# Both broadcasts of a group of head pairs in one place, the last reciprocals ahead of operand tiles, and two side-by-side products that end one after the other

## The chip, the cores and the metric

The kernel runs on one core of one Trainium2 chip. Its time is the device time of one execution in microseconds (us), as the median of several runs. PE is the matrix engine (TensorE), DVE the vector engine, ACT the scalar engine, POOL the GpSimd engine; SP only issues DMAs here. Each engine works through its own instructions in order, and semaphores tie the engines together.

## The reference

Attention with a tanh cap on the scores, then a gated layer with RMS normalisation, then a second layer with a leaky activation:

```
scores = cap * tanh(q @ k.T / 8 / cap)        # 2 batches x 12 heads, 448 x 64
attn   = exp(scores - max); attn /= attn.sum(-1) + 1e-9
x      = (attn @ v) as 896 x 768
xn     = x / sqrt(mean(x * x) + 1e-6) * rms_g
y      = (silu(xn @ w_gate) * (xn @ w_val)) @ w_out        # 768 -> 1536 -> 768
h      = y @ w_in                                          # 768 -> 2048
out    = (max(h, 0) + alpha * min(h, 0)) @ w_out2          # 2048 -> 768
```

## The kernel before

The attention comes first. Heads go two by two: 12 **pairs** (6 for each batch element), and each pair takes two **bursts**, numbered 0 to 23, so that pair i has bursts 2i and 2i + 1. A burst is: PE makes the scores of two key blocks (`qk`, L189), ACT applies tanh and exp (`soft`, L199 and L201, output `pt`), and PE multiplies the `pt` of the burst before with the values (`pv`, L212, into `oo`). Beside this skeleton two tables of numbers, `early` (filled by `ahead`, emitted between `qk` and `soft`) and `later` (filled by `at`, emitted at the end of the burst), say in which burst each other step is emitted.

A pair is divided by its softmax sums in these steps. In burst 2i + 2 PE sums the exponentials (`sums`, L228, into the PSUM bank `u`), DVE copies the unnormalised output (`evac_o`, L254, tile `ee`) and the sums (`evac_u`, L262, tile `us`), and SP spreads the sums over partitions by two small DMAs (tile `gt`). Two pairs make a **group**; `recip` (L269) works on a whole group with four small DVE instructions (L274 to L281: add, reciprocal, high part `th`, remainder `tl`) and two DMAs that bring the result into the rows `r`. `norm` (L306) is PE's broadcast of such a row over the partitions (L310, `rps<-r`) and DVE's product (L311, `xf<-ee,rps`). `norm` always used the bank `r`, but for the two at burst 23 and the one of pair 10, which share out `r` and `u`. POOL squares and adds up each finished pair (`square`, L292 to L300).

For the first batch element `rms_sum` (PE, L330), `rms_root` (ACT, L335, which loads a table for the square root) and `rms_tail` (DVE, L338, a reciprocal over 448 columns) give the RMS factor, and `xnorm` (L351 to L358) makes the high and low parts `xh`, `xl` of the operand tiles that the first products of the next stage read.

The products of the dense layers run as three-term sums of high and low parts: `wh` (ACT, L120) and `wl` (DVE, L124) are a weight block, and seven block products P1 to P7 per group of output columns follow Strassen's and Winograd's scheme; POOL forms the sums S1 to S4 of weight blocks (L115). `product` (L378) does one. `products` (L390) does the first two kinds, P5 and then P6, for two output groups side by side, so that the low operand part is read last. P6 and P7 share PSUM banks: between them DVE takes P6 out (`u2`, L562, `b<-s,c`), and P7 (operand T3, from `later_operands`) goes on in the same banks. A second planner (`do(slot, rank, ...)`) hangs such steps on the slots of the dense stage.

Pairs 8, 9 and 10 are divided at the very end, and pair 11 is divided without the detour over DMA (`norm_now`, with bank `r` for its sums).

Of the kernel before, what the change touches and what calls it, by code (L numbers as in the profile page):

```python
# [54 lines left out]
def attn_moe_kernel(ctx: ExitStack, tc: tile.TileContext, units, qk_in, v, sel, w, gvec, alpha, cap, out):  # L55
# [87 lines left out]
    def sum3(lay, g):  # L143

        w_sum((lay, g, "S3"), (lay, g, "A22"), (lay, g, "S2"), ALU.subtract, home=(lay, g, "A21"))
# [5 lines left out]
    def sum4(lay, g):  # L151

        w_sum((lay, g, "S4"), (lay, g, "A12"), (lay, g, "S2"), ALU.subtract, home=(lay, g, "A12"))
# [115 lines left out]
    def recip(n):  # L269
        t = gt.pop(n)  # L270
        w = 2 * len(members[n])
        m = slice(0, w * RP)
        f = sb.tile([4 * RP, S // RP], F32, tag="gf", name="gf")
        nc.vector.scalar_tensor_tensor(  # L274
            out=f[m], in0=t[m, 0], scalar=eps_t[m], in1=t[m, 1], op0=ALU.add, op1=ALU.add
        )
        nc.vector.reciprocal(out=f[m], in_=f[m])
        th = sb.tile([4 * RP, S // RP], F32R, tag="th", name="th")
        tl = sb.tile([4 * RP, S // RP], F32R, tag="tl", name="tl")
        nc.vector.tensor_copy(th[m], f[m])  # L280
        nc.vector.tensor_tensor(out=tl[m], in0=f[m], in1=th[m], op=ALU.subtract)  # L281
        rr = r2[n % 2]
        for r0, x in ((0, th), (32, tl)):
            row = rr[r0:r0 + w].rearrange("r (p s) -> r p s", p=RP)
            nc.sync.dma_start(out=row.bitcast(F32), in_=x[m].bitcast(F32))
# [27 lines left out]
    def norm_now(i):  # L313

        b, p = divmod(i, NP)
        u = sb.tile([P, S], F32, tag="us", name="us")
        nc.vector.tensor_scalar_add(u, us.pop(i)[:, :S], eps_t)
        nc.vector.reciprocal(out=u, in_=u)
        nc.vector.tensor_tensor(out=xf[b][:, p, :], in0=oo.pop(i)[:, :S], in1=u, op=ALU.mult)
        square(i)  # L320
# [5 lines left out]
    def rms_sum(b):  # L326
        ms = ms_of[b] = ps_o.tile([P, 512], F32, tag="o", name="ms")
        parts = s2.pop(b)
        for n, t in enumerate(parts):
            nc.tensor.matmul(ms[:, :S], ones, t, start=n == 0, stop=n == len(parts) - 1)  # L330
# [6 lines left out]
    def rms_tail(b):  # L337
        nc.vector.reciprocal(out=rstd[b], in_=rstd[b])  # L338
# [9 lines left out]
    def xnorm(i, late=None):  # L348
        b, p = divmod(i, NP)
        x = xf[b][:, p, :]  # L350
        nc.vector.scalar_tensor_tensor(  # L351
            out=x, in0=x, scalar=g_t[:, p:p + 1], in1=rstd[b], op0=ALU.mult, op1=ALU.mult
        )
        if b == 0:
            h, l = first_operand("B21" if p >= K3 else "B11")
            if late is None:
                nc.vector.tensor_copy(h[:, p % K3, :], x)
                nc.vector.tensor_tensor(out=l[:, p % K3, :], in0=x, in1=h[:, p % K3, :], op=ALU.subtract)  # L358
            else:
                nc.scalar.copy(h[:, p % K3, :], x)  # L360
                late.append((l[:, p % K3, :], x, h[:, p % K3, :]))

    def lows(late):
        for o, x, h in late:
            nc.vector.tensor_tensor(out=o, in0=x, in1=h, op=ALU.subtract)
        del late[:]
# [16 lines left out]
    def products(pss, us, name):  # L383

        xh, xl = oper[name]
        mm = [(p, x, k) for k in range(K3) for p, x in ((h_t, xh), (l_t, xh))] + [(h_t, xl, k) for k in range(K3)]
        for n, (wt, x, k) in enumerate(mm):
            for ps, u in zip(pss, us):
                for r in range(2):
                    nc.tensor.matmul(  # L390
                        ps[:, r, :S], wt[u][:, r * K3 + k, :], x[:, k, :], start=n == 0, stop=n == len(mm) - 1,
                        skip_group_check=True,
                    )


    with tc.manual_schedule():
# [39 lines left out]
        def at(n, fn, *a):  # L436
            later.setdefault(n, []).append((fn, a))

        def ahead(n, fn, *a):
            early.setdefault(n, []).append((fn, a))  # L440
# [6 lines left out]
        for i in range(NPAIR):  # L447
            e = 2 * i
            at(e, prep, i + 1)
            at(e, load_raw, i + 2)  # L450
            at(e, load_v, i + 1)
            if i > 0:
                at(e, sums, i - 1)
                if i % 2 == 1 and i > 2:
                    at(e, recip, (i - 3) // 2)
                if i - 2 in range(len(conv)):
                    at(e, w_bits, conv[i - 2])
                    if i - 2 < len(conv) - RAW:
                        at(e, w_next, conv[i - 2])
                if i == 10:  # L460
                    at(e, rms_tail, 0)
                at(e, evac_o, i - 1)
                at(e, evac_u, i - 1)
            if i in range(3, last):
                ahead(e + 1, norm, i - 3)
                at(e + 1, square, i - 3)
            if i - 1 in range(len(conv)):
                at(e + 1, w_top, conv[i - 1])
        for i in (last - 3, last - 2):
            ahead(NA - 1, norm, i, "ru"[i - last + 3])  # L470
        for n, j in ((6, 0), (8, 1), (18, 6), (22, 7)):
            at(n, w_hi, conv[j])
            if j < 7:
                at(n + 1, w_lo, conv[j])
        for n, fn, g in ((13, sum1, 0), (15, sum1, 1), (17, sum2, 0), (19, sum2, 1), (21, sum3, 0)):
            at(n, fn, "g", g)
        at(18, rms_sum, 0)
        at(19, rms_root, 0)
        for m in range(3):
            at((21, 21, 22)[m], xnorm, m)  # L480
        for n in range(NA):
            i, b = bursts[n]
            for g in (2 * b, 2 * b + 1):
# [15 lines left out]
        def ct(name):  # L499
            return xpool.tile([P, 2, S], F32, tag="ct", name=name, bufs=2)  # L500
# [3 lines left out]
        def first_sum(g, home):  # L504

            c21[g] = home
            nc.scalar.copy(home, pa[g][:, :, :S])  # L507
# [4 lines left out]
        square(last - 3)  # L512
        square(last - 2)
        recip(len(members) - 1)
        late = []
        xnorm(NP - 3, late)
        lows(late)
        norm_now(last)
        for g in (1, 0):
            (sum3 if g else sum4)("g", g)  # L520
        product(pa[0], ("g", 0, "A11"), "B11", True, rows=(0,))
        norm(last - 1, "u")
        square(last - 1)
        product(pa[0], ("g", 0, "A11"), "B11", True, rows=(1,))
        xnorm(NP - 2, late)
        xnorm(NP - 1, late)
        lows(late)
        rms_sum(B - 1)
        first_sum(0, ct("c21"))
        rms_root(B - 1)  # L530
        w_hi(("g", 0, "S1"))
        w_lo(("g", 1, "A12"))
        sum4("g", 1)
        rms_tail(B - 1)
        product(pa[1], ("g", 1, "A11"), "B11", True)
        first_sum(1, ct("c21"))
        w_hi(("g", 1, "S1"))
        c11 = [spare[B - 1][:, :2], xpool.tile([P, 2, S], F32, tag="B22l", name="c11")]
# [256 lines left out]
        def later_operands(n0, steps):  # L795
            for name, at_sum, at_hi, out, a, b in steps:
                if a is not None:
                    do(n0 + at_sum, 5, tt, out, a, b, ALU.subtract)
                do(n0 + at_hi, 5, operand, name, out)
                do(n0 + at_hi + 1, 2, operand_low, name, out)  # L800

        b11, b12, b21, b22 = x0[:, lo3], x1[:, lo3], x0[:, hi3], x1[:, hi3]
        later_operands(0, (
# [212 lines left out]
```

## Time and profile before

| | us |
|---|---|
| median of 3 runs | 592.72 (592.49 to 594.05) |
| profiled execution, its own time | 599.0 |
| span of the profiled execution | 597.2 |

PE is busy for 97% of the span, DVE for 66%, ACT for 57%, POOL for 19%. The mean granted clock of PE is 0.992 of full speed. A share of PE that high leaves some 19 us in which PE does nothing, 5.4 us of it before the first matmul and 4.3 us behind the last. So the places in the middle where PE waits, or runs at a lower clock, are few, and they can be read one by one. All stretches below are in us from the span's start, in the time of this one profiled execution.

### The profile page before, as it was taken

How to read it: one execution, taken by the hardware profiler on the slowest of the kernel's cores; microseconds unless marked ns; L12 is line 12 of the kernel's file. 1: busy time of each engine (PE TensorE's matmuls, PEld its weight loads, DVE VectorE, ACT ScalarE, POOL GpSimd, SP SyncE). 2: the span in 40 equal slices, each digit the busy share in tenths (PEclk: the TensorE clock that was granted, in tenths of full speed). 3: DMA queues.
4: the chain of work that ended last, by engine and by line, in shares of the span. 5: the costliest groups of instructions: out<-in, count | busy, mean ns of one | idle time of the engine just before them, and what ended most of it. 6: DMA issues, size and time to landing. Idle time of an engine off the chain costs nothing.

```text
span 597.2 us, 7299 instructions
## 1 busy us (share of the span) xinstructions
PE 577.8 (97%) x2925; PEld 472.8 (79%) x2925; DVE 394.1 (66%) x425; ACT 341.7 (57%) x392; POOL 114.9 (19%) x60
## 2 busy tenths in 40 slices
PE   6999999899899999999999999999999999999997
PEld 3444444389699999999999999999889889999996
DVE  5568869897997696769661643969986877504100
ACT  6998889456545544447634344486775986332101
POOL 0014545410046242310000053401441000000000
PEclk9999999799999999999999999999999999999999
DMA  7655420300136334114631653004321344431002
GB/s 253 220 194 157 139 71 19 137 25 1 26 133 212 106 106 159 53 60 152 210 115 46 224 200 106 0 1 150 120 101 54 128 137 159 158 145 53 1 1 92
DMA packets 16506, 66.05 MB, mean 111 GB/s; under 512 B 3544, under 2 KB 4056, under 8 KB 16472
## 3 DMA queue, kind: packets, MB, share of 16 engines
q1 hardware_dynamic: 16184, 65.45, 32.1%
q8 instruction: 23, 0.38, 0.3%
q0 software_dynamic: 144, 0.13, 0.1%
q14 instruction: 11, 0.09, 0.1%
q10 hardware_dynamic: 144, 0.00, 0.0%
HBM read 62.66 MB, written 2.75 MB: 110 GB/s over the span
## 4 chain that ended last, share of the span: by engine, by line
PE 82%; DVE 11%; DMA 3%; issue 2%; ACT 2%; SPq 0%; ACTq 0%; DVEq 0%
PE s L378 19%; PE m L378 14%; PE s L652 6%; PE s L654 6%; PE s L656 6%; PE m L652 6%; PE m L656 5%; PE m L654 5%; PE oo L212 5%; PE s L189 4%; DVE b L562 2%; PE us L228 2%; DVE wl L124 1%; PE m L390 1%; PE s L390 1%
## 5 line engine op out<-in xcount | busy, mean ns | idle before, releaser
L124 DVE TENSOR_TENSOR wl<-wt,wh 128x768 fp32r<-128x768 f32 x98 | 105.5, 1083 | 94.4 <-ACT wh L120 94.3
L115 POOL TENSOR_TENSOR wt<-wt 128x768 f32<-128x768 f32 x40 | 92.3, 2312 | 264.4 <-DVE wt L107 148.5
L120 ACT CAST wh<-wt 128x768 fp32r<-128x768 f32 x98 | 81.2, 832 | 89.7 <-PE s L654 24.5
L103 ACT CAST top<-raw 128x768 f16<-128x768 bf16 x68 | 72.6, 1076 | 46.1 <-DVE wt L107 39.8
L107 DVE SCALAR_TENSOR_TENSOR wt<-raw,top 128x768 uint32<-128x768 uint32 x68 | 69.7, 1029 | 1.5 <-ACT top L103 1.5
L378 PE MATMUL s<-xh,wh 128*128 128x448 f32 x222 | 58.3, 370 | 0.9 <-DVE b L562 0.9
L378 PE MATMUL s<-xl,wh 128*128 128x448 f32 x222 | 57.8, 368 | 0.8 <-DVE xl L562 0.8
L378 PE MATMUL s<-xh,wl 128*128 128x448 f32 x222 | 57.7, 368 | 0.0
L652 PE MATMUL s<-ks,wh 128*128 128x448 f32 x176 | 50.6, 367 | 0.8 <-DVE b L893 0.8
L656 PE MATMUL s<-ks,wl 128*128 128x448 f32 x176 | 50.4, 366 | 0.0
L378 PE MATMUL m<-xh,wh 128*128 128x448 f32 x174 | 45.6, 370 | 2.1 <-ACT b L507 1.5
L199 ACT ACTIVATE pt<-s,cinv 128x896 f32<-128x896 f32 (+1 forms) x48 | 41.2, 907 | 9.8 <-PE s L189 9.5
L378 PEld LDWEIGHTS s<-xh,wh 128*128 128x128 f32 x222 | 41.4, 188 | 6.4 <-ACT wh L120 1.2
L652 PE MATMUL m<-ks,wh 128*128 128x448 f32 x160 | 45.9, 368 | 0.5 <-DVE b L562 0.5
L656 PE MATMUL m<-ks,wl 128*128 128x448 f32 x160 | 45.7, 367 | 0.0
L378 PEld LDWEIGHTS s<-xl,wh 128*128 128x128 f32 x222 | 41.6, 188 | 5.2 <-DVE xl L562 1.2
L378 PE MATMUL m<-xh,wl 128*128 128x448 f32 x174 | 45.3, 368 | 0.0
L378 PE MATMUL m<-xl,wh 128*128 128x448 f32 x174 | 45.3, 368 | 0.0
L378 PEld LDWEIGHTS s<-xh,wl 128*128 128x128 f32 x222 | 41.7, 188 | 4.1
L212 PE MATMUL oo<-pt,vt 128*64 128x448 f32 x192 | 42.9, 569 | 0.8 <-ACT pt L201 0.7
L654 PE MATMUL s<-b,wh 128*128 128x448 f32 x144 | 41.4, 366 | 0.0
L654 PE MATMUL m<-b,wh 128*128 128x448 f32 x144 | 41.2, 367 | 0.0
(138 smaller groups left out, 910.9 us busy)
## 6 DMA issues: line engine op xcount, KB each, us to landing
raw<-w_in SPq DMA_DIRECT2D x68, 768.0 KB
rw<-qk_in SPq DMA_DIRECT2D x11, 480.0 KB
vt<-v_in SPq DMA_DIRECT2D x12, 256.0 KB
out<-o SPq DMA_DIRECT2D x5, 448.0 KB
out<-o SPq DMA_DIRECT2D x2, 224.0 KB
gt<-us SPq DMA_DIRECT2D x22, 3.5 KB
rw<-qk_in SPq DMA_DIRECT2D x1, 256.0 KB
rw<-qk_in SPq DMA_DIRECT2D x1, 224.0 KB
```

The costliest lines, as they stand in the source:

```text
L103: nc.scalar.copy(top_of[u].bitcast(F16)[:, 1::2], raw_t[u].bitcast(BF16)[:, 4:4 * UW + 4:4])
L107: nc.vector.scalar_tensor_tensor(out=f_t[u].bitcast(U32), in0=raw_t.pop(u).bitcast(U32)[:, 1:2 * UW + 1:2], scalar=13, in1=top_of.pop(u), ...
L115: nc.gpsimd.tensor_tensor(out=t, in0=f_t[a], in1=f_t[b], op=op)
L120: nc.scalar.copy(h_t[u], f_t[u].rearrange("p (k m) -> p k m", m=P))
L124: nc.vector.tensor_tensor(out=l_t[u], in0=f_t[u].rearrange("p (k m) -> p k m", m=P), in1=h_t[u], op=ALU.subtract)
L189: nc.tensor.matmul(s[:, h, :S], kt[rows, c:c + P], qt[rows, :S], start=m == 0, stop=m == 2, skip_group_check=True,)
L199: nc.scalar.activation(out=t[:, n:n + w], in_=st.pop((i, g))[:, :w, :S], func=AF.Tanh, scale=cinv)
L212: nc.tensor.matmul(oo[i][h * D:h * D + D, :S], vv[:, 2 * c + h, :], t[:, n, :], start=c == 0, stop=c == 3, skip_group_check=True,)
L378: nc.tensor.matmul(ps[:, r, :S], lhs, rhs, start=first and n == 0, stop=n == len(mm) - 1, skip_group_check=True,)
L652: nc.tensor.matmul(dst[l], wh[:, o, :], xh[l], start=first, stop=False)
L654: nc.tensor.matmul(dst[l], wh[:, o, :], xl[l], start=False, stop=False)
L656: nc.tensor.matmul(dst[l], wl[:, o, :], xh[l], start=False, stop=fin)
```

## The change

Four edits. First, `norm` and `square` of both pairs of a group are emitted in the same burst, the one that the second pair had before, with the broadcasts in the banks `r` and `u`. Second, the end of the attention is put in another order: `rms_tail` of the first batch element stands behind the copies of burst 20 instead of ahead of them, `recip` of pairs 8 and 9 is in burst 21 instead of 22 and ahead of the `xnorm` steps, which are spread over bursts 21, 22 and 23 (two in 21 and one in 22 before); behind the last burst all three `xnorm` steps of pairs 3 to 5 stand behind `norm_now`, and the RMS sum of the second batch element is half a product later. POOL's sums move: S2 of group 1 from burst 19 to 21, S3 of group 0 behind the attention. Third, in `products` the last pass, with the low operand part, does one output group after the other instead of in turn. Fourth, the low part of T3 gets rank 0.5 instead of 2 in its slot.

```diff
@@ -383,14 +383,15 @@
     def products(pss, us, name):
 
         xh, xl = oper[name]
-        mm = [(p, x, k) for k in range(K3) for p, x in ((h_t, xh), (l_t, xh))] + [(h_t, xl, k) for k in range(K3)]
-        for n, (wt, x, k) in enumerate(mm):
-            for ps, u in zip(pss, us):
-                for r in range(2):
-                    nc.tensor.matmul(
-                        ps[:, r, :S], wt[u][:, r * K3 + k, :], x[:, k, :], start=n == 0, stop=n == len(mm) - 1,
-                        skip_group_check=True,
-                    )
+        both = [(ps, u) for ps, u in zip(pss, us)]
+        mm = [(p, x, k, m) for k in range(K3) for p, x in ((h_t, xh), (l_t, xh)) for m in both]
+        mm += [(h_t, xl, k, m) for m in both for k in range(K3)]
+        for n, (wt, x, k, (ps, u)) in enumerate(mm):
+            for r in range(2):
+                nc.tensor.matmul(
+                    ps[:, r, :S], wt[u][:, r * K3 + k, :], x[:, k, :], start=n < len(both),
+                    stop=x is xl and k == K3 - 1, skip_group_check=True,
+                )
 
 
     with tc.manual_schedule():
@@ -451,19 +452,18 @@
             at(e, load_v, i + 1)
             if i > 0:
                 at(e, sums, i - 1)
-                if i % 2 == 1 and i > 2:
+                if i % 2 == 1 and 2 < i < last:
                     at(e, recip, (i - 3) // 2)
                 if i - 2 in range(len(conv)):
                     at(e, w_bits, conv[i - 2])
                     if i - 2 < len(conv) - RAW:
                         at(e, w_next, conv[i - 2])
-                if i == 10:
-                    at(e, rms_tail, 0)
                 at(e, evac_o, i - 1)
                 at(e, evac_u, i - 1)
-            if i in range(3, last):
-                ahead(e + 1, norm, i - 3)
-                at(e + 1, square, i - 3)
+            if i % 2 == 0 and 2 < i < last:
+                for j in range(2):
+                    ahead(e + 1, norm, i - 4 + j, "ru"[j])
+                    at(e + 1, square, i - 4 + j)
             if i - 1 in range(len(conv)):
                 at(e + 1, w_top, conv[i - 1])
         for i in (last - 3, last - 2):
@@ -472,12 +472,14 @@
             at(n, w_hi, conv[j])
             if j < 7:
                 at(n + 1, w_lo, conv[j])
-        for n, fn, g in ((13, sum1, 0), (15, sum1, 1), (17, sum2, 0), (19, sum2, 1), (21, sum3, 0)):
+        for n, fn, g in ((13, sum1, 0), (15, sum1, 1), (17, sum2, 0), (21, sum2, 1)):
             at(n, fn, "g", g)
         at(18, rms_sum, 0)
         at(19, rms_root, 0)
+        at(20, rms_tail, 0)
+        at(21, recip, len(members) - 2)
         for m in range(3):
-            at((21, 21, 22)[m], xnorm, m)
+            at(21 + m, xnorm, m)
         for n in range(NA):
             i, b = bursts[n]
             for g in (2 * b, 2 * b + 1):
@@ -512,27 +514,27 @@
         square(last - 3)
         square(last - 2)
         recip(len(members) - 1)
+        norm_now(last)
+        sum4("g", 0)
+        sum3("g", 0)
         late = []
-        xnorm(NP - 3, late)
-        lows(late)
-        norm_now(last)
-        for g in (1, 0):
-            (sum3 if g else sum4)("g", g)
         product(pa[0], ("g", 0, "A11"), "B11", True, rows=(0,))
         norm(last - 1, "u")
         square(last - 1)
         product(pa[0], ("g", 0, "A11"), "B11", True, rows=(1,))
-        xnorm(NP - 2, late)
-        xnorm(NP - 1, late)
+        for m in range(NP - 3, NP):
+            xnorm(m, late)
         lows(late)
+        first_sum(0, ct("c21"))
+        product(pa[1], ("g", 1, "A11"), "B11", True, rows=(0,))
         rms_sum(B - 1)
-        first_sum(0, ct("c21"))
         rms_root(B - 1)
         w_hi(("g", 0, "S1"))
         w_lo(("g", 1, "A12"))
         sum4("g", 1)
+        sum3("g", 1)
         rms_tail(B - 1)
-        product(pa[1], ("g", 1, "A11"), "B11", True)
+        product(pa[1], ("g", 1, "A11"), "B11", True, rows=(1,))
         first_sum(1, ct("c21"))
         w_hi(("g", 1, "S1"))
         c11 = [spare[B - 1][:, :2], xpool.tile([P, 2, S], F32, tag="B22l", name="c11")]
@@ -797,7 +799,7 @@
                 if a is not None:
                     do(n0 + at_sum, 5, tt, out, a, b, ALU.subtract)
                 do(n0 + at_hi, 5, operand, name, out)
-                do(n0 + at_hi + 1, 2, operand_low, name, out)
+                do(n0 + at_hi + 1, 0.5 if name == "T3" else 2, operand_low, name, out)
 
         b11, b12, b21, b22 = x0[:, lo3], x1[:, lo3], x0[:, hi3], x1[:, hi3]
         later_operands(0, (
```

On DVE, in bursts 20 to 22, there stood before (`ee` and `us` are the copies of pair 9, `spare` the RMS reciprocal, `xf<-ee,rps` the product of pair 7, `xf<-xf,g_t,spare` to `xl` an `xnorm`, `gf` the start of `recip` for pairs 8 and 9):

```order
L338 RECIPROCAL spare_899<-spare_899 128x448
L254 COPY ee_939<-oo_889 128x448
L262 COPY us_941<-us_929 128x448
L311 TENSOR_TENSOR xf_93<-ee_776,rps_956 128x448
L351 SCALAR_TENSOR_TENSOR xf_92<-xf_92,g_t_81,spare_899 128x448
L357 CAST xh_973<-xf_92 128x448
L358 TENSOR_TENSOR xl_974<-xf_92,xh_973 128x448
L351 SCALAR_TENSOR_TENSOR xf_92<-xf_92,g_t_81,spare_899 128x448
L357 CAST xh_973<-xf_92 128x448
L358 TENSOR_TENSOR xl_974<-xf_92,xh_973 128x448
L274 SCALAR_TENSOR_TENSOR gf_1011<-gt_861,eps_t_83 64x28
L277 RECIPROCAL gf_1011<-gf_1011 64x28
```

And now, from the same two copies on:

```order
L254 COPY ee_932<-oo_886 128x448
L262 COPY us_934<-us_923 128x448
L338 RECIPROCAL spare_893<-spare_893 128x448
L311 TENSOR_TENSOR xf_93<-ee_699,rps_950 128x448
L311 TENSOR_TENSOR xf_93<-ee_770,rps_953 128x448
L274 SCALAR_TENSOR_TENSOR gf_971<-gt_861,eps_t_83 64x28
L277 RECIPROCAL gf_971<-gf_971 64x28
L280 CAST th_974<-gf_971 64x28
L281 TENSOR_TENSOR tl_975<-gf_971,th_974 64x28
L351 SCALAR_TENSOR_TENSOR xf_92<-xf_92,g_t_81,spare_893 128x448
L357 CAST xh_981<-xf_92 128x448
L358 TENSOR_TENSOR xl_982<-xf_92,xh_981 128x448
```

The copies of pair 9 come ahead of the RMS reciprocal, the products of pairs 6 and 7 follow each other, and the whole of `recip` stands ahead of the first `xnorm`, not behind the second.

On PE, in burst 9 (the second pair of the first group), there stood before the last scores, one broadcast and the values:

```order
L189 MATMUL s_463<-hi_338 128x448
L189 MATMUL s_463<-hi_338,lo_339 128x448
L189 MATMUL s_463<-lo_339,hi_338 128x448
L310 MATMUL rps_467<-r2_0_88,sel_t_87 128x448
L212 MATMUL oo_474<-pt_419,vt_344 64x448 x4
```

And now:

```order
L189 MATMUL s_458<-hi_338 128x448
L189 MATMUL s_458<-hi_338,lo_339 128x448
L189 MATMUL s_458<-lo_339,hi_338 128x448
L310 MATMUL rps_462<-r2_0_88,sel_t_87 128x448
L310 MATMUL rps_465<-r2_0_88,sel_t_87 128x448
L212 MATMUL oo_472<-pt_414,vt_344 64x448 x4
```

The broadcast that stood in burst 7 at this place comes here, ahead of the other one; the same holds for bursts 13, 17 and 21.

On DVE, between P6 and P7, there stood before (`b0` is a gate product, `wl_1309` the low part of S3 of group 0, `b3` the two outputs of `u2`, `xl_1312` the low part of T3, `xf_92<-xf_92` the sum for T4):

```order
L562 TENSOR_TENSOR b0_1300<-c11_1167,b0_1300 128x448
L124 TENSOR_TENSOR wl_1309<-wt_444,wh_1305 128x768
L562 TENSOR_TENSOR b3_1353<-s_1304,c21_1135 128x896
L124 TENSOR_TENSOR wl_1355<-wt_533,wh_1351 128x768
L562 TENSOR_TENSOR xl_1312<-xf_93,xh_1311 128x1344
L562 TENSOR_TENSOR xf_92<-xf_92 128x1344
```

And now:

```order
L564 TENSOR_TENSOR b0_1300<-c11_1167,b0_1300 128x448
L124 TENSOR_TENSOR wl_1309<-wt_439,wh_1305 128x768
L564 TENSOR_TENSOR xl_1312<-xf_93,xh_1311 128x1344
L564 TENSOR_TENSOR b3_1354<-s_1304,c21_1130 128x896
L124 TENSOR_TENSOR wl_1356<-wt_533,wh_1351 128x768
L564 TENSOR_TENSOR xf_92<-xf_92 128x1344
```

The low part of T3 moves ahead of the first `u2`, so it no longer stands between the two. SP's queue has the same rows in the same order as before.

## Rows read from the trace of the kernel before

**Rows 1.** The page: span, and busy time by engine.

```profile
span 597.2 us, 7299 instructions
...
PE 577.8 (97%) x2925; PEld 472.8 (79%) x2925; DVE 394.1 (66%) x425; ACT 341.7 (57%) x392; POOL 114.9 (19%) x60
```

**Rows 2.** Waits of PE: engine, line, releaser, then total us, times, longest.

```profile
PE rps L310 <- DMA r<-tl: 3.9, 3, 2.8
PE m L378 <- ACT b L507: 1.5, 1, 1.5
```

**Rows 3.** Timeline of PE: start, duration, instruction; idle before it in brackets.

```profile
52.36 0.45 PE L310 MATMUL rps<-r,sel_t 128*128 128x448 f32 x1 [0.41 <-DMA r<-tl]
...
60.62 0.36 PE L310 MATMUL rps<-r,sel_t 128*128 128x448 f32 x1
...
69.66 0.44 PE L310 MATMUL rps<-r,sel_t 128*128 128x448 f32 x1 [0.69 <-DMA r<-tl]
...
94.03 0.55 PE L228 MATMUL us<-pt,half 128*32 128x448 f32 x2
...
97.26 1.72 PE L212 MATMUL oo<-pt,vt 128*64 128x448 f32 x8 [0.73 <-ACT pt L201]
...
108.09 1.08 PE L310 MATMUL rps<-r,sel_t 128*128 128x448 f32 x2 [2.79 <-DMA r<-tl]
109.11 3.26 PE L212 MATMUL oo<-pt,vt 128*64 128x448 f32 x8
...
150.82 0.85 PE L378 MATMUL s<-xh,wh 128*128 128x448 f32 x3 [0.86 <-DVE b L562]
...
153.07 0.88 PE L378 MATMUL s<-xl,wh 128*128 128x448 f32 x3 [0.77 <-DVE xl L562]
...
160.09 0.85 PE L378 MATMUL m<-xh,wh 128*128 128x448 f32 x3 [0.59 <-DVE c L562]
```

**Rows 4.** Stretches: length, busy by engine (count), PE clock, DMA share, GB/s.

```profile
106.00:108.00 2.00, 0.00 (x0) 0.00 (x0) 1.93 (x4) 1.95 (x3) 0.00 (x0) 0.72 0.07 9
108.09:117.53 9.44, 9.44 (x34) 3.26 (x34) 7.15 (x11) 2.61 (x5) 6.59 (x4) 0.70 0.36 130
432.00:434.00 2.00, 0.88 (x4) 0.82 (x5) 1.68 (x2) 2.00 (x4) 0.88 (x1) 1.00 0.78 233
```

**Rows 5.** Timeline of DVE, columns as in PE's.

```profile
59.23 0.62 DVE L262 COPY us<-us 128x448 f32<-128x448 f32 x1 [1.03 <-PE us L228]
...
93.66 2.94 DVE L338 RECIPROCAL spare<-spare 128x448 f32<-128x448 f32 x1
...
97.00 0.60 DVE L262 COPY us<-us 128x448 f32<-128x448 f32 x1
97.52 0.60 DVE L311 TENSOR_TENSOR xf<-ee,rps 128x448 f32<-128x448 f32 x1
...
101.18 2.25 DVE L351 SCALAR_TENSOR_TENSOR xf<-xf,g_t,spare 128x448 f32<-128x448 f32 x1
...
104.44 0.23 DVE L274 SCALAR_TENSOR_TENSOR gf<-gt,eps_t 64x28 f32<-64x28 f32 x1
...
106.44 0.67 DVE L351 SCALAR_TENSOR_TENSOR xf<-xf,g_t,spare 128x448 f32<-128x448 f32 x1
...
149.59 1.09 DVE L562 TENSOR_TENSOR b<-s,c 128x896 f32<-128x896 f32 x1 [3.44 <-PE s L390]
...
151.46 1.55 DVE L562 TENSOR_TENSOR xl<-xf,xh 128x1344 fp32r<-128x1344 f32 x1
```

**Rows 6.** Stretches with DVE's busy time, columns as in the stretches above.

```profile
97.60:150.68 53.08, 49.57 (x238) 34.78 (x234) 45.72 (x62) 32.41 (x43) 13.11 (x8) 0.94 0.12 46
150.68:160.09 9.41, 7.91 (x37) 6.56 (x37) 9.38 (x9) 4.57 (x5) 0.00 (x0) 1.00 0.00 0
```

**Rows 7.** Timeline of POOL while DVE's row at 101.18 ran.

```profile
100.73 2.22 POOL L115 TENSOR_TENSOR wt<-wt 128x768 f32<-128x768 f32 x1
```

**Rows 8.** Timeline of SP's queue: the second half of the reciprocals leaves.

```profile
105.96 0.58 SPq L285 DMA_DIRECT2D r<-tl  x1
```

## The prediction

> **What bounds the kernel now.** The page comes first: PE is busy 577.8 of 597.2 us [rows 1]. The change adds no matmul and takes none away, so it can only give back time in which PE stands or runs slowly. The table of PE's waits is next. Its largest entry in the middle of the kernel is the broadcast of the reciprocals, which waits for its DMA three times, 3.9 us in all, 2.8 of it once [rows 2]. The timeline of PE then shows where. The first two are 0.41 and 0.69 us, in bursts 11 and 15; the third, 2.79, stands at the end of the attention, ahead of 108.09. Three more waits follow when the dense layer starts: 0.86, 0.77 and 0.59 us, all for DVE [rows 3].
>
> The third wait has a second price. The granted clock, 1.00 elsewhere, is 0.72 on average over 106 to 108, in which PE does nothing, and 0.70 over 108.09 to 117.53, in which it is busy throughout [rows 4]: 1.00 stands for 2.4 GHz, and the lower level, 1.2 GHz, is half of it. The lost share is (1 - 0.70) x 9.44 = 2.8 us; the eight value matmuls at 109.11 take 3.26 us and the same eight at 97.26 take 1.72 [rows 3]. A wait of 1.5 us for ACT, ended at 433.1, left the clock at 1.00 [rows 2, 4].
>
> The timeline of DVE says why the third wait exists. DVE starts the reciprocals of pairs 8 and 9 only at 104.44, with an RMS reciprocal of 2.94 us and two operand tiles in front of them [rows 5]. The second DMA leaves at 105.96 [rows 8], and the broadcast starts 2.1 us later.
>
> **The change part by part.**
>
> *Broadcasts side by side.* The four broadcasts of the first pairs of a group move two bursts back, from 52.36 to 60.62 for the third pair, 8.3 us [rows 3]. The DMAs were late by 0.41 and 0.69, so both waits go: **1.10 us**. PE, ACT and DVE pass this on, since ACT and DVE wait for PE in these bursts (1.03 us of it in the row at 59.23 [rows 5]). The new wait is that of the second broadcast for its bank, u, which the copy of the softmax sums must have left. That copy ends at 59.85 and the broadcast stands at 60.62, so 0.77 us are spare, and DVE had waited 1.03 ahead of the copy: it may come 1.8 us late before PE waits. Behind the broadcast PE has the value matmuls of the burst, and ACT waits for what follows. I take the new wait as nothing in bursts 9, 13 and 17.
>
> *The end of the attention.* The copy of the sums of pair 9 no longer stands behind the RMS reciprocal. PE ends those sums at 94.58 [rows 3]; with 0.60 for the copy it ends at 95.2 instead of 97.60 [rows 5]. From there DVE is what the next 55 us hang on: from 97.60 to 150.68, the end of the first `u2`, it is busy 45.72 of 53.08 us [rows 6]. The change adds three things to this list: the RMS reciprocal, 2.94; the product of pair 6, 0.60 by the row of pair 7; and the low part of T3, 1.55, which goes ahead of `u2` [rows 5]. Together 50.81 us, so without a pause `u2` would end at 95.18 + 50.81 = 146.0.
>
> There will be pauses, and POOL is one source. It now has four pieces of work in burst 21 (two squares, an addition, S2 of group 1) while DVE runs the reciprocals and the next operand tile. At 101.18 the scaling of one tile took DVE 2.25 us, where 106.44 shows it at 0.67 [rows 5]. It ended just after POOL's weight sum, which ran from 100.73 to 102.95 [rows 7]; so 1.58 us were lost beside one POOL instruction. Two POOL instructions come into the stretch, so the bounds of the extra are 0 and 3.2 us; I take the middle, 1.6, since the row shows the loss for one kind of DVE instruction and one kind of POOL's. `u2` then ends at **147.6**.
>
> The GPSIMD Engine Reference of the Trainium skill (section Specifications) says that POOL shares its SBUF interfaces with VectorE, and that DVE instructions with two SBUF inputs or in a two-port mode contend with it. By that rule this very change has a price: of the four small instructions of `recip` three are of those kinds, and each could wait out a piece of POOL's new run. Had the rule no hold here, the sum below would gain the 1.6 us back (7.3 instead of 5.7); with all of it, it loses another 1.6 (4.1). The trace agrees in the row at 101.18.
>
> The reciprocals get clear of this in time. They start at 95.2 + 2.94 + 2 x 0.60 = 99.3, 5.1 us sooner than 104.44, and even with 3.2 us lost they leave 1.9 us sooner. What is late next at PE's place is the bank u: the copy of the sums of pair 10, behind the first operand tile on DVE. I expect PE to wait about 1 us there instead of 2.79, about as long as the wait at 433.1, so I take the clock to stay up. The 1 us and the 2.8 us of clock are no terms of their own, because DVE ends later than PE in this stretch.
>
> *T3 ahead, and the last pass group by group.* From 150.68 to 160.09 DVE is busy without a pause (9.38 of 9.41 [rows 6]), and PE's last wait in this group ends at 160.09. Without the low part of T3 the stretch has 7.86 us: 147.6 + 7.86 = 155.4. That is **4.6 us** sooner. The 0.77 goes by itself, as its releaser now stands in front. The other order of the last pass frees the first bank six matmuls ahead of the end instead of two. PE does the 30 matmuls from 153.07 to 159.50 in 6.43 us, so four are 0.86, just the wait at 150.82. But `u2` is kept by DVE in this sum, so I cost it at nothing; where DVE is early it is worth up to 0.86.
>
> Rearranged squares on ACT, POOL's sums and the `xnorm` steps behind the last burst are in DVE's list already or wait for it. The RMS sum of the second batch element, half a product later, hides in PE's queue, which still has five half products behind it.
>
> **Sum.** 1.1 + 4.6 = 5.7 us. The profiled execution took 599.0 and would take 593.3. It is 6.3 above the median of the runs, which holds for before and after alike; 592.7 - 5.7 = **587.0 us**.
>
> **The rivals.**
>
> *PE alone decides (13%).* If POOL costs DVE less than I think, only PE's own work counts. From 105.30 to 160.09 PE loses 2.79 + 0.86 + 0.77 + 0.59 = 5.0 us idle and 2.8 to the clock. All of it back, with the 1.1: 8.9 us, 583.8. For it speaks that most pauses of DVE in the old stretch were waits for a PE that stood or ran at the low clock; against it that DVE is busy 86% there.
>
> *The clock falls all the same (16%).* The copy of pair 10's sums is late enough that PE stands almost as long as before, with 2.8 us of wait and 2.8 of clock. PE reaches the place of 160.09 at 105.3 + 47.0 + 5.6 = 157.9, 2.2 us sooner: 3.3 with the first term, 589.4. For it speaks the 2.25 of the row at 101.18; against it that the copy needs only PE's sums and one tile.
>
> *DVE gives it back (12%).* POOL's 3.2 in full, and half of the 3.9 us of other pauses (7.36 idle less 3.44 ahead of `u2` [rows 5, 6]): `u2` ends at 151.1, P3 starts at 159.0, 2.2 us in all, 590.5. Nothing would be left but small ends.
>
> *Slower: bank u in every group (3%).* The second broadcast of bursts 9, 13, 17 and 21 waits for the copy of the sums. The cover is 1.8 us; from there each us is paid four times, so at a copy 3.7 us late the gain is gone, and at 4.0 us it is 595.8. In these bursts POOL does twice the squares, which speaks for it; but `recip` stands in the others, so DVE has less to do.
>
> The forecast has 55%. The last 1% is for waits that I don't see, ACT's `pt` at 97.26 (0.73 us) among them, which the change doesn't touch.
>
> **How the numbers follow.** What can be told from no change is about 0.3%, 1.8 us. The forecast, PE alone and the fallen clock are all faster by more; so are half of the cases around 590.5. That makes 0.90 faster, 0.06 within, 0.04 slower. The range goes from 584.3, inside the first rival, to 590.6, which takes in the fallen clock and the middle of the third rival; some 16% lie outside.
>
> **What would show it.** The broadcasts of pairs 2 and 4 have no idle time ahead of them; the two at the last burst start some 1 us behind the last scores, and the granted clock is 1.00 through the sums and values that follow. DVE has no gap of more than a us between the copy of pair 9's sums and `u2`. The copy ends ahead of the RMS reciprocal; the low part of T3 is there before PE wants it. Wrong would be a clock below 0.9 around 110, a broadcast that waits in bursts 9, 13 or 17, or a DVE that waits for PE ahead of `u2` as it did for 3.44 us.

## The result, and the profile after

The changed kernel takes 587.36 us, median of 21 runs (586.83 to 593.63), against 594.05 for the kernel before in 21 runs beside it (592.34 to 598.99). The ratio is 0.990, interval 0.9877 to 0.9923: 1.0% less, some 5.9 us (4.6 to 7.3); the two medians lie 6.7 apart. The forecast was 587.0. Its profiled execution took 593.33 us against 599.0.

The page after, span and busy time:

```profile
span 591.6 us, 7296 instructions
...
PE 575.7 (97%) x2925; PEld 472.6 (80%) x2925; DVE 392.5 (66%) x425; ACT 341.2 (58%) x392; POOL 109.4 (18%) x60
```

The span is 5.6 us shorter, PE's busy time 2.1 (575.7 against 577.8): 3.5 us of idle time went, and 2.1 of matmul time with the same 2925 matmuls [rows 1]. The timeline of PE after, at the places of [rows 3] (start, duration, instruction, idle before it in brackets):

```profile
44.97 0.57 PE L310 MATMUL rps<-r,sel_t 128*128 128x448 f32 x2
...
61.32 0.57 PE L310 MATMUL rps<-r,sel_t 128*128 128x448 f32 x2
...
105.07 0.37 PE L310 MATMUL rps<-r,sel_t 128*128 128x448 f32 x1
105.68 0.47 PE L310 MATMUL rps<-r,sel_t 128*128 128x448 f32 x1 [0.25 <-DVE us L262]
106.08 1.72 PE L212 MATMUL oo<-pt,vt 128*64 128x448 f32 x8
...
116.06 0.44 PE L310 MATMUL rps<-r,sel_t 128*128 128x448 f32 x1 [1.42 <-DMA r<-tl]
...
147.07 0.85 PE L378 MATMUL s<-xh,wh 128*128 128x448 f32 x3 [0.43 <-ACT wh L120]
...
154.87 0.85 PE L378 MATMUL m<-xh,wh 128*128 128x448 f32 x3
```

The paired broadcasts (x2) of bursts 9 and 13 have no idle ahead of them. At the last burst, where PE had waited 2.79 us, stands 0.25 for bank u, and the eight value matmuls behind it take 1.72, not 3.26. The 0.77 and the 0.59 at the start of the dense layers are gone; 0.43 is left of the 0.86, and it is now for ACT. One row is new: the broadcast of pair 10 waits 1.42 us for its reciprocals, which it did not before.

Stretches after, to set beside [rows 4, 6] (length; busy time and count of PE, PEld, DVE, ACT, POOL; clock; DMA share; GB/s):

```profile
94.98:146.92 51.94, 49.33 (x247) 34.97 (x243) 51.08 (x66) 34.54 (x45) 15.02 (x10) 1.00 0.12 47
...
106.00:108.00 2.00, 1.92 (x11) 0.60 (x12) 1.93 (x5) 1.96 (x2) 0.00 (x0) 1.00 0.03 4
108.00:118.00 10.00, 8.58 (x43) 4.95 (x44) 9.69 (x11) 1.88 (x4) 6.18 (x4) 1.00 0.18 64
```

The granted clock stays at 1.00 in this execution, through the wait of 1.42 too. DVE is busy 51.08 of the 51.94 us from its copy of pair 9's sums to the end of the first `u2`, where it had been 45.72 of 53.08. The timelines of DVE and then of POOL, at the two places where the reciprocals run:

```profile
94.36 0.62 DVE L262 COPY us<-us 128x448 f32<-128x448 f32 x1 [1.04 <-PE us L228]
...
98.76 0.61 DVE L274 SCALAR_TENSOR_TENSOR gf<-gt,eps_t 64x28 f32<-64x28 f32 x1
99.40 0.32 DVE L277 RECIPROCAL gf<-gf 64x28 f32<-64x28 f32 x1
99.76 0.50 DVE L280 CAST th<-gf 64x28 fp32r<-64x28 f32 x1
...
100.39 1.56 DVE L351 SCALAR_TENSOR_TENSOR xf<-xf,g_t,spare 128x448 f32<-128x448 f32 x1
101.99 1.91 DVE L357 CAST xh<-xf 128x448 fp32r<-128x448 f32 x1
...
109.97 1.12 DVE L274 SCALAR_TENSOR_TENSOR gf<-gt,eps_t 32x28 f32<-32x28 f32 x1
111.12 0.32 DVE L277 RECIPROCAL gf<-gf 32x28 f32<-32x28 f32 x1
111.47 0.82 DVE L280 CAST th<-gf 32x28 fp32r<-32x28 f32 x1
112.32 1.77 DVE L281 TENSOR_TENSOR tl<-gf,th 32x28 fp32r<-32x28 f32 x1
...
145.84 1.08 DVE L564 TENSOR_TENSOR b<-s,c 128x896 f32<-128x896 f32 x1
```

```profile
101.43 2.22 POOL L115 TENSOR_TENSOR wt<-wt 128x768 f32<-128x768 f32 x1
...
109.57 1.48 POOL L300 TENSOR_TENSOR s<-s,sq 128x448 f32<-128x448 f32 x1 [5.91 <-ACT sq L298]
111.12 1.12 POOL L300 TENSOR_TENSOR s<-s,sq 128x448 f32<-128x448 f32 x1
112.21 1.84 POOL L115 TENSOR_TENSOR wt<-wt 128x768 f32<-128x768 f32 x1
```

The operand cast takes 1.91 beside POOL's sum at 101.43, and 0.39 where POOL is quiet (below). The add, the cast and the remainder of pair 10's reciprocals run beside POOL's work from 109.57 on and take 1.12, 0.82 and 1.77; the RECIPROCAL between them takes 0.32 both times. Each of the three ends just behind one of POOL's instructions: at 111.09, 112.29 and 114.09, where POOL's end at 111.05, 112.24 and 114.05. So here it was the rest of POOL's instruction that such a DVE instruction lost, however small its own work. The second DMA leaves behind the remainder, and with it the broadcast comes late.

**How spans are compared.** Two things differ between executions of one and the same kernel. The changed kernel profiled again has 298 matmuls in the 60 us from 225 to 285, the execution above 292, both at granted clock 1.00:

```profile
225.00:285.00 60.00, 60.00 (x292) 54.50 (x291) 46.16 (x50) 31.15 (x38) 10.72 (x5) 1.00 0.31 105
```

```profile
225.00:285.00 60.00, 60.00 (x298) 55.61 (x297) 47.02 (x50) 31.17 (x38) 8.78 (x5) 1.00 0.34 113
```

From start to start that is 0.207 or 0.203 us (the counts take in a matmul or two that the window's ends cut), 4.5 us over the 235 us from 165 to 400. And two of the profiles made (the first of the changed kernel and that of the last experiment) lose some 1.8 us at the start, where the first value matmuls take 3.26 instead of 1.72 us. So below I compare stretches up to the first matmul of P3, which end before most of the dense layers, and medians of the runs that share a chip. "End stretch" is the time from the start of burst 21's first broadcast to the first matmul of P3: 63.9 us before (96.16 to 160.09), and 58.8 in each of three profiles after (the 58.6 of some expectations counts from the second broadcast).

### The profile page after: what moved, and what is told of

Read it like the earlier page. It is cut to its first block, busy times and chain, and to the rows that moved or that the text cites. A ratio compares the mean times of both kernels' runs of the same rounds, so it can differ in the third digit from the quotient of the medians.

```text
span 591.6 us, 7296 instructions
## 1 busy us (share of the span) xinstructions
PE 575.7 (97%) x2925; PEld 472.6 (80%) x2925; DVE 392.5 (66%) x425; ACT 341.2 (58%) x392; POOL 109.4 (18%) x60
## 4 chain that ended last, share of the span: by engine, by line
PE 83%; DVE 10%; DMA 2%; issue 2%; ACT 2%; SPq 0%; ACTq 0%; DVEq 0%
PE s L378 18%; PE m L378 15%; PE s L656 6%; PE s L658 6%; PE s L654 6%; PE s L189 6%; PE oo L212 6%; PE m L654 6%; PE m L658 6%; PE m L656 6%; PE us L228 3%; DVE xf L351 1%; DVE b L564 1%; DVE wl L124 1%; DVE b L895 1%
## 5 line engine op out<-in xcount | busy, mean ns | idle before, releaser
L124 DVE TENSOR_TENSOR wl<-wt,wh 128x768 fp32r<-128x768 f32 x98 | 105.7, 1085 | 94.3 <-ACT wh L120 94.2
L115 POOL TENSOR_TENSOR wt<-wt 128x768 f32<-128x768 f32 x40 | 89.5, 2243 | 259.3 <-DVE wt L107 143.7
L107 DVE SCALAR_TENSOR_TENSOR wt<-raw,top 128x768 uint32<-128x768 uint32 x68 | 67.7, 999 | 3.6 <-ACT top L103 3.6
```

What stands on the lines that cost most here:

```text
L107: nc.vector.scalar_tensor_tensor(out=f_t[u].bitcast(U32), in0=raw_t.pop(u).bitcast(U32)[:, 1:2 * UW + 1:2], scalar=13, in1=top_of.pop(u), ...
L115: nc.gpsimd.tensor_tensor(out=t, in0=f_t[a], in1=f_t[b], op=op)
L124: nc.vector.tensor_tensor(out=l_t[u], in0=f_t[u].rearrange("p (k m) -> p k m", m=P), in1=h_t[u], op=ALU.subtract)
```

## The experiments

**The parts alone.** Theory: edit 2 carries the gain, since the place of the last reciprocals ends the wait and DVE does the rest. Rivals: the parts add up, or the last pass alone does it.

Edit 1 alone, the broadcasts in pairs, on the kernel before:

```
-            if i in range(3, last):
-                ahead(e + 1, norm, i - 3)
-                at(e + 1, square, i - 3)
+            if i % 2 == 0 and 2 < i < last:
+                for j in range(2):
+                    ahead(e + 1, norm, i - 4 + j, "ru"[j])
+                    at(e + 1, square, i - 4 + j)
```

> Only the side-by-side broadcasts (first edit) on the kernel before. My theory: the two waits ahead of the broadcasts in bursts 11 and 15 go, 1.1 us by the idle times, up to 2 us if the start-to-start distances count; but in burst 21 the second broadcast must wait for the copy of pair 9, which still stands behind the RMS reciprocal, so 0.6 us come back there, and the third wait (2.8 us, then a clock of 0.5) stays. Sum: 0.5 to 1.5 us faster than before. Rival that only the end of the attention counts: no change at all. Rival that bank u costs in every group: slower, with waits for the copy of the sums in bursts 9, 13 and 17.

Measured: 592.24 us, ratio 0.9964 (0.9932 to 0.9996). The two waits are gone and burst 21's broadcast starts at 94.64 instead of 96.16. The 0.6 us that I expected back at bank u in burst 21 did not come: neither broadcast there has idle time ahead of it. The third wait stays at 2.68 and the clock falls behind it. So edit 1 is worth 1.5 us there, more than the 1.1 of the rows.

Edit 2 alone, the end of the attention and POOL's sums:

```
-                if i % 2 == 1 and i > 2:
+                if i % 2 == 1 and 2 < i < last:
-                if i == 10:
-                    at(e, rms_tail, 0)
...
+        at(20, rms_tail, 0)
+        at(21, recip, len(members) - 2)
-            at((21, 21, 22)[m], xnorm, m)
+            at(21 + m, xnorm, m)
```

> Only the second edit (RMS reciprocal behind the copies, reciprocals of pairs 8 and 9 in burst 21 ahead of the tiles, the end behind the last burst, POOL's sums) on the kernel before; broadcasts, products and T3 as before. My theory (DVE decides the end of the attention): third wait 0 to 0.5 us, clock 1.00 throughout, 3.5 to 4.5 us faster than before; the waits of 0.4 and 0.7 us in bursts 11 and 15 stay, and the waits for DVE at the start of the dense layer stay or grow, since DVE has less of a lead on PE there. Rival that PE alone decides: 2.8 us of wait and 2.8 us of clock come back in full, 5.5 us or more.

Measured: 589.36 us, ratio 0.9909 (0.9872 to 0.9947), and an end stretch of 58.3 us instead of 63.9. PE waits at neither of the last broadcasts. That is 5.6 us less, the rival's size and not the 3.5 to 4.5 that I expected: 63.9 less the third wait (2.79) and the lost clock (2.8) is 58.3. DVE's list did not decide here, as DVE waits 2.32 us for PE ahead of `u2`. The three waits of the dense start remain (timelines of DVE and PE):

```profile
144.30 1.09 DVE L562 TENSOR_TENSOR b<-s,c 128x896 f32<-128x896 f32 x1 [2.32 <-PE s L390]
...
145.54 0.84 PE L378 MATMUL s<-xh,wh 128*128 128x448 f32 x3 [0.86 <-DVE b L562]
147.78 0.86 PE L378 MATMUL s<-xl,wh 128*128 128x448 f32 x3 [0.79 <-DVE xl L562]
154.80 0.84 PE L378 MATMUL m<-xh,wh 128*128 128x448 f32 x3 [0.51 <-DVE c L562]
```

Edits 3 and 4 alone, the last pass and the rank of T3's low part:

```
-                do(n0 + at_hi + 1, 2, operand_low, name, out)
+                do(n0 + at_hi + 1, 0.5 if name == "T3" else 2, operand_low, name, out)
```

> Only the third and fourth edits (last pass group by group, low part of T3 first) on the kernel before. DVE has 3.4 us of idle time ahead of the takeout of P6 there, so my theory gives back the waits of 0.86 and 0.77 us and part of the 0.59: 1.6 to 2.0 us faster. Rival that PE's wait there is set by DVE's queue and not by the order in which the banks end: below 0.8 us.

Measured: 592.54 us, ratio 0.9964 (0.9924 to 1.0003). The 0.86 and the 0.77 are gone, the third wait of 2.77 and the low clock remain. End stretch 60.1; beside the 62.3 of edit 1 alone, which has a like dip of the clock and 0.2 for one broadcast more in it, that is 2.0 less.

Edits 1 and 2 without 3 and 4:

> The changed kernel without the third and fourth edits. My theory: with the end of the attention sped up, DVE is what PE waits for, so the low part of T3 still has to be done and only its place changes: 0.5 to 1.0 us slower than the changed kernel (about 588 us where that takes 587.4). Rival that the edits add up: what they give alone is lost here in full, 1.6 to 2.0 us.

Measured: 590.87 us, ratio 0.9943 (0.9911 to 0.9975), end stretch 60.7. The waits are those of the changed kernel at the attention's end (0.25 and 1.42) and those of before at the dense start (0.86, 0.79, 0.50), and DVE idles 1.83 ahead of `u2`. Edits 3 and 4 thus bring 1.9 us here too, the rival's figure and not the 0.5 to 1.0 that I expected: the low part of T3 fills a pause that DVE would have had.

The parts do not add up. Edit 1 brings 1.5 to 1.9 us early, but with it the end stretch of edit 2 grows from 58.3 to 60.7, of which one broadcast more explains 0.2: 2.1 are given back. Where, is the question for the rest.

**Is it the place of the reciprocals?** The changed kernel, with those of pairs 8 and 9 back in burst 22 behind two operand tiles:

```
-        at(21, recip, len(members) - 2)
-            at(21 + m, xnorm, m)
+            at((21, 21, 22)[m], xnorm, m)
```

> The changed kernel, but the reciprocals of pairs 8 and 9 stand in burst 22 again, behind two operand tiles (the tiles in bursts 21, 21, 22 as before); all else of the change stays. My theory (the place of these reciprocals decides on the third wait and the clock): the wait ahead of the last two broadcasts is 2.5 us or more again, the granted clock falls to 0.5 behind it, and PE loses 1.8 to 2.8 us there; DVE's lead makes up some of it, so 2 to 4 us slower than the changed kernel. Rival (the copies ahead of the RMS reciprocal are what matters): below 1 us slower, wait below 1.5 us.

Measured: 592.08 us, ratio 0.9934 (0.9896 to 0.9971); the changed kernel beside it 587.87, 0.9862 (0.9813 to 0.9911). The expectations for that one:

> The changed kernel again, on the chip of the three that follow, as their measure. Every theory: about 1% below the kernel before; broadcast of pair 10 late by about 1.4 us, DVE without a pause from the copies of pair 9 to the takeout of P6.

The end stretch is 63.1 us instead of 58.8. PE's timeline and two stretches:

```profile
107.47 1.09 PE L310 MATMUL rps<-r,sel_t 128*128 128x448 f32 x2 [3.94 <-DMA r<-tl]
108.49 3.26 PE L212 MATMUL oo<-pt,vt 128*64 128x448 f32 x8
```

```profile
106.00:108.00 2.00, 0.53 (x2) 0.50 (x2) 1.52 (x3) 1.25 (x2) 0.00 (x0) 0.72 0.06 9
108.00:110.00 2.00, 2.00 (x6) 0.53 (x6) 1.71 (x5) 1.07 (x2) 0.34 (x1) 0.50 0.00 0
```

Wait and low clock come back together: the place of `recip`, ahead of the operand tiles or behind two of them, decides both, 4.2 us of the end. The two lines moved as one, so what the spread of the tiles alone does isn't shown.

**What makes pair 10 late?** Theory: POOL's work of burst 21, raised by the change from three instructions (4.7 us) to four (5.3), stretches DVE's instructions. The changed kernel with S2 of group 1 back in burst 19, twice:

```
-        for n, fn, g in ((13, sum1, 0), (15, sum1, 1), (17, sum2, 0), (21, sum2, 1)):
+        for n, fn, g in ((13, sum1, 0), (15, sum1, 1), (17, sum2, 0), (19, sum2, 1)):
```

> The changed kernel with POOL's S2 of group 1 in burst 19 as before, where DVE waits for PE anyway. My theory (DVE decides, and POOL's work beside it costs DVE time): the cast of the first tile, 1.91 us in the changed kernel, takes about 0.4 to 1.0; the reciprocals of pair 10 start over 1 us sooner; the broadcast of pair 10 waits below 0.3 us instead of 1.4; 1 to 2 us faster than the changed kernel. Rival (POOL's presence costs DVE nothing that PE waits for): within 0.5 us of it.

Measured: 586.48 us, ratio 0.9845 (0.979 to 0.99). The cast takes 0.40, both waits are gone, and the end stretch is 55.8, 3.0 less than beside it, where 1 to 2 were expected. The second time:

> S2 of group 1 back in burst 19, a second look. If POOL's work in burst 21 is what delays the reciprocals: both waits gone, 55.8 us from the broadcast of burst 21 to P3, 2.5 to 3 us below the changed kernel beside it. If the first look was chance: within 1 us of the changed kernel, and the stretch at 58.6.

Measured: 588.05, ratio 0.9896 (0.9856 to 0.9937), end stretch again 55.8. The stretch is settled; the intervals of the medians overlap with those of the changed kernel.

The changed kernel with the broadcasts and squares of pairs 6 and 7 in bursts of their own:

```
-            if i % 2 == 0 and 2 < i < last:
+            if i % 2 == 0 and 2 < i < last - 1:
...
+            if i in (last - 2, last - 1):
+                ahead(e + 1, norm, i - 3)
+                at(e + 1, square, i - 3)
```

> The changed kernel, but pairs 6 and 7 get their broadcasts apart, in bursts 19 and 21 as before; the first three groups stay side by side. My theory: what the pairing gives it gives in bursts 11 and 15, and in burst 21 it only adds a product and a square to the busiest stretch of DVE and POOL; so the broadcast of pair 10 no longer waits and this is 1 to 2 us faster than the changed kernel. Rival (the pairing is worth the same in each group): 0.3 us or more slower.

Measured: 588.7 us, ratio 0.9845 (0.9786 to 0.9904), no wait at the broadcasts, end stretch 56.0. The timed runs don't tell it from the changed kernel beside it; the stretch is 2.9 shorter. Yet its cast is as long as before, and only the reciprocals of pair 10 are shorter:

```profile
99.94 1.91 DVE L357 CAST xh<-xf 128x448 fp32r<-128x448 f32 x1
...
107.92 0.23 DVE L274 SCALAR_TENSOR_TENSOR gf<-gt,eps_t 32x28 f32<-32x28 f32 x1
...
109.38 0.18 DVE L281 TENSOR_TENSOR tl<-gf,th 32x28 fp32r<-32x28 f32 x1
```

Both edits together:

> S2 of group 1 back in burst 19 and the broadcasts and squares of pairs 6 and 7 in bursts of their own again. If the two remedies take away one and the same wait, the stretch to P3 stays at 55.5 to 56 us as with either alone, 2.5 to 3 us below the changed kernel. If each takes away contention of its own, 53 to 54.5 us, and 4 to 5 us below.

Measured: 584.12 us (583.76 to 588.43), ratio 0.9834 (0.9803 to 0.9865), and the end stretch 56.05, as with either alone (55.8 and 56.0): they take away one and the same loss. Its DVE where the changed kernel has 1.91, 1.12, 0.82 and 1.77:

```profile
99.45 0.39 DVE L357 CAST xh<-xf 128x448 fp32r<-128x448 f32 x1
...
106.78 0.23 DVE L274 SCALAR_TENSOR_TENSOR gf<-gt,eps_t 32x28 f32<-32x28 f32 x1
107.04 0.32 DVE L277 RECIPROCAL gf<-gf 32x28 f32<-32x28 f32 x1
107.39 0.17 DVE L280 CAST th<-gf 32x28 fp32r<-32x28 f32 x1
107.60 0.18 DVE L281 TENSOR_TENSOR tl<-gf,th 32x28 fp32r<-32x28 f32 x1
```

The three stretched instructions of the reciprocals lost 0.89 + 0.65 + 1.59 us to POOL and the cast 1.52, 4.65 in all; 3 of it reach P3, as DVE now waits some 0.97 for ACT's square root and 0.69 for the sums of pair 11. The 3 are those of the reciprocals, since with the broadcasts apart the cast's loss stays and the stretch is as short. What the remedies share is when these reciprocals start: 0.40 us behind POOL's additions in the changed kernel (109.97 against 109.57), and 0.80, 0.26 and 0.91 ahead of them with S2 back, with the broadcasts apart and with both. The changed kernel, once more on the same chip:

> The changed kernel once more, as the measure for the three runs beside it. Between 586.8 and 588.5 us, some 0.986 to 0.991 of the kernel before; the two waits of the broadcasts of pairs 9 and 10 at 0.25 and 1.4 us, and 58.6 to 58.9 us from the broadcast of burst 21 to the first matmul of P3.

Measured: 589.54 us, above the 586.8 to 588.5 expected; ratio 0.9918 (0.9889 to 0.9948), end stretch 58.8. The intervals of this and of the version with both edits don't meet: that version beats both kernels. Of the 5.4 us between the two medians the end stretch shows 2.7; where the rest comes from isn't shown.

**Does PE's wait of 1.42 cost anything itself?** The changed kernel, with the broadcast of pair 10 behind both halves of the first product:

```
-        product(pa[0], ("g", 0, "A11"), "B11", True, rows=(0,))
+        product(pa[0], ("g", 0, "A11"), "B11", True)
         norm(last - 1, "u")
         square(last - 1)
-        product(pa[0], ("g", 0, "A11"), "B11", True, rows=(1,))
```

> The broadcast of pair 10 and its squares stand behind both halves of the first product instead of between them; POOL's sums as in the changed kernel. If PE's wait of 1.4 us at that broadcast is itself on the path: the wait is gone, and the stretch to P3 falls from 58.7 to some 57.3 us. If DVE's list decides, as predicted: the wait is gone, the stretch stays at 58.5 to 58.9, and the 1.4 us come back as waits of PE at P6, P7 or P3.

Measured: 591.52 us, ratio 0.9923 (0.9888 to 0.9958), end stretch 58.8. The wait is gone, and it is back further on (timeline of PE):

```profile
116.30 0.37 PE L310 MATMUL rps<-r,sel_t 128*128 128x448 f32 x1
...
131.51 0.68 PE L391 MATMUL m<-xh,wl 128*128 128x448 f32 x2 [0.68 <-DVE wl L124]
132.37 0.67 PE L391 MATMUL m<-xh,wl 128*128 128x448 f32 x2 [0.19 <-DVE wl L124]
...
147.07 0.85 PE L378 MATMUL s<-xh,wh 128*128 128x448 f32 x3 [1.05 <-ACT wh L120]
```

0.68 + 0.19 + (1.05 - 0.43) = 1.49 for the 1.42. DVE's list sets the end, wherever PE does its waiting.

## Why the prediction was right

The size came out: 5.7 us forecast, 5.9 by the ratio. Part of that is luck. Both terms were too small, 1.1 against 1.9 and 4.6 against 5.1 (63.9 to 58.8), so the profiles show 7.0; that the timed runs show less is taken up below. The steps:

- *Broadcasts side by side, 1.10: the term was too small.* In seven profiles with all broadcasts in pairs, those with the slower start left out, the first of burst 21 stands at 94.2 to 94.6, and at 96.2 to 96.5 in three with them apart: 1.9 us. Between the broadcasts of bursts 9 and 17 the gain is 1.65 (34.34 us from 43.60 to 77.94 before; 32.69 from 44.97 to 77.66 after) where the rows had 0.41 + 0.69. Idle time in the profile counts from the modelled end of the matmul before. Undisturbed, the broadcast starts 0.20 behind the last scores, whose own row says 0.37, so each wait cost some 0.17 more than its bracket, and the broadcast behind it takes 0.45 instead of 0.36. The one of burst 7, at 35.34, stood 0.38 behind the scores and shows no bracket at all. That no new wait came in bursts 9, 13 and 17 held.
- *DVE's list.* The copy was to end at 95.2 and `u2` at 147.6, 52.4 us; they came at 94.98 and 146.92, 51.9 (the ends themselves agree by chance, as the late start hid the 1.9 of the broadcasts). On top of the 50.81 of the sum the forecast had 1.6 for POOL, and 1.13 came: 0.27 more busy time and 0.86 idle. So the rival *DVE gives it back*, with 3.2 and half of the old pauses, did not come. That the list decides, and PE's waits are only where it shows, was the step most in doubt; for the changed kernel the last experiment bears it out, with 1.42 us moved and none gained. In edit 2 alone and in the remedied versions it does not: there DVE waits for PE or ACT.
- *The reciprocals.* Start at 99.3 forecast, 98.76 measured. PE's wait at bank u was to be 1 us and was 0.25; the clock stayed up. So the rival in which the clock falls was wrong, because the copy came in time; and with `recip` put back, wait and low clock return.
- *POOL.* I put its price on the reciprocals of pairs 8 and 9 and the tile behind them. They paid 3.1 there (add 0.38, cast 0.33, scaling 0.89, cast of the tile 1.52, each against the shortest row of its kind); as much again, 3.1, fell on those of pair 10, which the prediction had not looked at, and made the wait of 1.42. Of such losses the kernel before had 5.6 us in its stretch already and the changed one 6.8, so what is new is 1.2 by these rows and 0.3 by DVE's busy time. What the prediction missed is which of them reaches PE. The page GPSIMD Engine Reference of the Trainium skill (section Specifications) names the DVE instructions that contend with POOL: those with two SBUF inputs or in a two-port mode. The trace agrees: add, cast and remainder were stretched, the RECIPROCAL between them was not (0.32 with and without POOL). Here one instruction lost up to 1.6 us.
- *T3 ahead.* From the end of `u2` to P3: 7.86 forecast, 7.95 measured. Counting the last pass at nothing can't be judged by itself: edits 3 and 4 were not run apart. Together they are worth 1.9 to 2.0, by filling the pause that DVE has ahead of `u2` without them (1.83).
- *PE alone decides, 583.8.* It fails by what POOL costs DVE at pair 10's reciprocals. The rival takes 7.8 us from the end stretch, which leaves 56.1; the versions without most of that cost have 55.8 to 56.05. The one with both edits has the ratio 0.9834, which on the median of 592.72 is 582.9.
- *Slower, bank u in every group.* No such wait came. Its sum had a slip: with each us beyond 1.8 paid four times, the 5.7 are gone at a copy 3.2 us late, not 3.7.

**How far the sizes agree.** In profiles with a usual start P3 came 7.0 us sooner (160.09 to 153.09), where the ratio says 5.9. The dip of the clock can account for the difference. These are the stretches behind the third wait in the kernel before (wait of 2.79, ended at 108.09) and then with edits 3 and 4 alone (2.77, ended at 108.29):

```profile
108.00:110.00 2.00, 1.91 (x6) 0.88 (x8) 1.35 (x4) 1.47 (x3) 0.00 (x0) 0.50 0.01 2
110.00:112.00 2.00, 2.00 (x8) 0.62 (x6) 1.90 (x5) 0.67 (x2) 1.65 (x2) 0.50 0.00 0
112.00:114.00 2.00, 2.00 (x8) 0.65 (x6) 1.37 (x2) 0.56 (x1) 2.00 (x2) 0.57 0.05 7
```

```profile
108.00:110.00 2.00, 1.71 (x6) 0.83 (x8) 1.64 (x4) 1.75 (x3) 0.00 (x0) 0.67 0.03 4
110.00:112.00 2.00, 2.00 (x6) 0.47 (x4) 1.90 (x5) 0.59 (x2) 1.72 (x2) 0.50 0.00 0
112.00:114.00 2.00, 2.00 (x14) 0.82 (x12) 1.37 (x2) 0.57 (x1) 2.00 (x2) 0.97 0.11 13
```

The lost shares make 1.00 + 1.00 + 0.86 = 2.9 us in the one and 0.66 + 1.00 + 0.06 = 1.7 in the other, after waits of one length. So the change is worth 7.0 against the long dip and 5.8 against the short one. The timed runs have no trace, but each has its mean granted clock on record: on average 0.9982 and 0.9990 in the two repeats of the changed kernel, and 0.9949 and 0.9954 in the runs of the kernel before beside them. That is 0.0035 of 590 us, an estimate of 2 us that the clock gives, nearer to the short dip.

The changed kernel isn't free of dips either. In its two repeats the clock stays up through the wait of 1.42 but falls once in the dense layers: behind waits of 1.13 and 0.52 us in the one, behind a wait of 2.04 for ACT in the other, and takes 1.7 us each time.

```profile
466.00:468.00 2.00, 1.64 (x5) 1.47 (x6) 2.00 (x4) 0.00 (x0) 0.00 (x0) 0.63 0.44 177
```

```profile
422.00:424.00 2.00, 1.88 (x7) 1.67 (x8) 1.57 (x3) 2.00 (x4) 0.00 (x0) 0.70 0.62 255
```

The prediction took the clock to stay up since a wait of 1.5 us had left it there. It did stay up, in all three profiles, but the length of a wait alone doesn't tell.

## What to carry to other kernels

Find the engine whose list ends last and add up its instructions through the change; a wait that is removed elsewhere only moves while that list is unchanged. When work is gathered in one place, ask what the engine beside it will be running at that moment: a remedy that let four small DVE instructions start ahead of POOL's additions brought 3 us more in the end stretch, where the whole change had brought 5. And count a wait on PE from start to start of its neighbours, as the brackets leave out part of it.

## What was not expected of the hardware

At granted clock 1.00 the same steady matmuls run at one of two paces, 0.203 or 0.207 us from start to start, whatever the kernel (from 225 to 285, seven of the profiles at the slower pace, seven at the faster). An execution needn't keep its pace: the kernel before has the slower one from 165 to 400 and the faster from 480 on, and the third profile of the changed kernel the other way about. From the first matmul of P3 to the end the fourteen profiles take 432.1 to 439.1 us, whatever the kernel, the dips of the clock included. That the spread of the timed runs (587 to 593 us for the changed kernel) has mostly the same source is likely, but not shown, as they have no trace. What sets the pace isn't visible in the traces.
